# Scores and tiled outputs of two batches in one stretch, later planned landings, halves in steps 1 and 2, an earlier load of wo, last rows in two parts: one change to a fused linear-attention and feed-forward kernel

## The chip, the cores and the metric

The kernel runs on one core of one Trainium2 chip. The metric is device time in microseconds, as the median of several executions; the spans in the profiles are some 1.5 to 2 us shorter. A comparison is a ratio of the two kernels' fast runs in the same rounds on the same chip, so it is not quite the ratio of the medians that are quoted beside it. A run over 1.5% above the fastest of its kernel counts as slow and is left out. "Faster" and "slower" mean by over 2%. The "granted clock" is the share of its full clock that TensorE was given, as the trace records it. The experiments ran on several chips, so I compare ratios to the kernel before, not microseconds.

## The reference

Four batches of 768 tokens, 8 heads of 48 columns. A gated linear attention feeds a gated feed-forward.

```python
f = 1 / (1 + exp(-f_logit))
for t in range(S):                                    # S = 768
    state = f[:, :, t, :, None] * state + einsum('bhd,bhe->bhde', k[:, :, t], v[:, :, t])
    y[:, :, t] = einsum('bhd,bhde->bhe', q[:, :, t], state)
x = y.transpose(0, 2, 1, 3).reshape(3072, 384)
out = (maximum(x @ w_gate, 0) * (x @ w_val)) @ w_out  # 384 -> 1536 -> 384
```

## The kernel before

The tokens are cut in six steps c of 128. For each step, and for two batches (a pair) at a time, the inputs f, k, q, v are loaded; ScalarE makes exponentials of the running sum of log f, GpSimd scales k and q with them ("hats"), both are transposed ("qkT"), TensorE makes the scores, VectorE masks them ("ptm"), and TensorE makes the output rows ("y") from masks, v and the state. All four batches of a step then form 512 columns for the feed-forward: 12 hidden blocks j, each with a gate and a value product of three matmuls, and the output projection.

The program is written by a planner. Every operation is added with its reads, writes, a duration and a priority; a list scheduler with a model of the DMA queues fixes one order for each engine and for the DMA queue, and each engine's program is written out in that order, with a wait for whatever an operation depends on:

```python
for op in order[name]:              # one engine's program
    for d in waits[op]:             # semaphores of what it depends on
        eng.wait_ge(...)
    ins = op.emit()
```

An operation on a PSUM bank gets one of eight; groups have limits, and an operation that opens several waits until so many are idle:

```python
pl = Plan({"bc": 2, "bc4": 4, "tp": 2, "s": 4, "y": 2, "kv": 1, "f": 4})
...                                                     # cut
idle = [s for s in slots if s["tile"] is None or all(o.start is not None for o in s["tile"].ops)]
return idle[:n] if len(idle) >= n else None
```

The early loads with their gates ("wo0@q1.0": not before q of step 1, pair 0, has landed), and the planned landing:

```python
flight = 3                                              # later loads: at most three in flight
first = ("f0.0 k0.0 q0.0 v0.0 f0.1 k0.1 q0.1 v0.1 wg0@f0.1 wv0 wg1@q0.1 wv1 wg2 wv2 f1.0@wv1 k1.0 q1.0 v1.0 wo0@q1.0 wo1 wo2 "
         "f1.1 k1.1 q1.1 v1.1").split()
...                                                     # cut, in transfers():
h[0].land = t + (0.6 if e == "SP" else 1.6)
```

Scores, one batch at a time: eight matmuls of 48 rows into two banks, two heads of a pair from partitions 0 and 64 on. The outputs of steps 0 to 2 are "tiled", 28 matmuls with 32 columns of weights each:

```python
sA, sB = Bank("s"), Bank("s")
def scores():
    for p in range(NP):
        for j, s in ((0, sA), (1, sB)):
            lo = 64 * j
            mm = te.matmul(s.ap[:, p * C:(p + 1) * C], tokens(c, b, 1, p, lo, lo + D), tokens(c, b, 0, p, lo, lo + D))
    return mm
chain("scores", "PE", scores, qk_(qi), [sA, sB], occ=0.34, lat=PE_L, prio=P + 5, opens=[sA, sB])
```

## Time and profile before

| | before |
|---|---|
| median time | 199.1 us (198.9 to 199.8) |
| profiled span | 197.6 us |
| TensorE busy | 185.2 us, 94% |
| granted clock in the profiled run | 1.00 |

The busy time of the engines by stretch, kernel before. Columns: stretch, its length, then busy us (and instructions) of TensorE, its weight loads, VectorE, ScalarE, GpSimd; last the granted clock, the DMA engines' share and GB/s.

```profile
0.00:50.00 50.00, 41.65 (x467) 24.97 (x472) 32.14 (x68) 28.63 (x65) 25.83 (x46) 1.00 1.07 207
50.00:130.00 80.00, 79.16 (x822) 43.81 (x832) 49.00 (x79) 54.53 (x122) 45.66 (x57) 1.00 0.99 201
```

The reader is to see two things: TensorE is idle 8.4 us in the first 50 and only 0.8 in the next 80; and the DMA engines' share is 1.07 and 0.99, so in both stretches the transfers fill them as well (the tool's share can come out a little above 1; I read both as full). (The trace of before lacks 23 of the 512-column matmuls; each leaves, by my estimate, about 0.05 us of seeming idle time, as a recorded one lasts 0.379 us and two starts around a missing one lie 2 x 0.217 us apart; so the true idle time in the second stretch is smaller still.)

### The profile page before, as it was taken

The page shows a single profiled execution, that of the slowest core. Times are in us where ns is not written, and L with a number is a line of the kernel's source. Part 1 is how long each engine was busy: PE and PEld are TensorE (multiplying, and loading weights), DVE is VectorE, ACT ScalarE, POOL GpSimd, SP SyncE. Part 2 cuts the span into 40 slices and gives each one's busy share as a digit, 9 for nine tenths or more (in the row PEclk, how much of TensorE's full clock was granted, in tenths as well). Part 3 has the DMA queues.
Part 4 walks back from the last instruction along what each step waited for, and adds up shares of the span by engine and source line. Part 5 has one row for each costly group of instructions (what it writes and reads, how often), then busy time and mean ns, then how long its engine had stood idle before and what let it go on. Part 6 is the DMA issues. An engine that isn't in the chain of part 4 may idle for free.

```text
span 197.6 us, 4229 instructions
## 1 busy us (share of the span) xinstructions
PE 185.2 (94%) x1681; PEld 102.3 (52%) x1705; DVE 105.7 (53%) x183; ACT 111.1 (56%) x237; POOL 76.3 (39%) x108
## 2 busy tenths in 40 slices
PE   6876896898999999999999999999999999999994
PEld 1344684455655554546455555544545555544562
DVE  7746873773829786576466455446247232443300
ACT  3667429761587768856646876377434434344311
POOL 8277003956376929684730645505400000000000
PEclk9999999999999999999999999999999999999999
DMA  5999999997999999997999979989361210111112
GB/s 136 251 285 206 206 197 222 204 207 152 203 239 242 224 190 205 189 241 135 195 214 196 215 169 181 213 167 250 71 134 62 61 40 0 43 40 40 40 75 85
DMA packets 118051, 31.73 MB, mean 161 GB/s; under 512 B 111120, under 2 KB 118032, under 8 KB 118032
## 3 DMA queue, kind: packets, MB, share of 16 engines
q1 hardware_dynamic: 114048, 27.93, 65.7%
q0 software_dynamic: 3984, 3.54, 11.2%
q8 instruction: 13, 0.21, 0.4%
q14 instruction: 6, 0.05, 0.1%
HBM read 25.95 MB, written 4.72 MB: 155 GB/s over the span
## 4 chain that ended last, share of the span: by engine, by line
PE 73%; DMA 14%; SPq 7%; POOL 2%; issue 1%; ACT 0%
PE ps L829 39%; PE ps L852 22%; SPq L474 7%; DMA q_in<-in_q_dram 7%; DMA wv<-in_moe_w_val_dram 4%; DMA f_in<-in_f_logit_dram 3%; PE ps L739 3%; PE ps L766 2%; PE ps L710 1%; PE ps L659 1%; PE ps L800 1%; PE ps L776 1%; PE ps L772 1%; POOL wg L494 1%; POOL hats L699 1%
## 5 line engine op out<-in xcount | busy, mean ns | idle before, releaser
L839 DVE TENSOR_TENSOR gT<-relu,ps 128x512 bf16<-128x512 bf16 (+1 forms) x78 | 50.0, 645 | 58.1 <-PE ps L829 45.1
L835 ACT ACTIVATE relu<-ps 128x512 bf16<-128x512 f32 (+1 forms) x78 | 43.6, 563 | 28.8 <-PE ps L829 28.5
L829 PE MATMUL ps<-xT,wv 128*128 128x512 bf16 (+1 forms) x225 | 57.5, 362 | 1.3 <-DMA wv<-in_moe_w_val_dram 0.7
L829 PE MATMUL ps<-xT,wg 128*128 128x512 bf16 (+1 forms) x220 | 56.7, 362 | 0.8 <-issue 0.2
L852 PE MATMUL ps<-wo,gT 128*128 128x384 bf16 x288 | 51.4, 326 | 0.1
L744 DVE TENSOR_TENSOR ptm<-ps,tri 128x512 bf16<-128x512 f32 x48 | 30.9, 685 | 11.7 <-PE ps L739 11.7
L852 PEld LDWEIGHTS ps<-wo,gT 128*128 128x128 bf16 x288 | 27.0, 98 | 18.7
L829 PEld LDWEIGHTS ps<-xT,wg 128*128 128x128 bf16 x234 | 21.7, 98 | 19.6
L829 PEld LDWEIGHTS ps<-xT,wv 128*128 128x128 bf16 x234 | 21.1, 98 | 20.5 <-DMA wv<-in_moe_w_val_dram 1.1
L696 POOL TENSOR_TENSOR hats<-k_in,expo 128x384 bf16<-128x384 f32 x20 | 20.0, 1002 | 28.4 <-ACT expo L669 15.5
L862 ACT ACTIVATE osb<-ps 128x384 f32<-128x384 f32 x24 | 11.8, 491 | 32.1 <-PE ps L852 32.0
L699 POOL TENSOR_TENSOR hats<-q_in,expo 128x384 bf16<-128x384 f32 x20 | 19.9, 1000 | 3.1 <-DMA q_in<-in_q_dram 2.7
L550 POOL TENSOR_TENSOR st<-ssum,dec 128x384 bf16<-128x384 f32 x16 | 13.5, 846 | 9.8 <-DVE ssum L548 9.8
L731 POOL CAST vpad<-v_in 128x384 bf16<-128x384 f32 x24 | 11.9, 507 | 3.6 <-DMA v_in<-in_v_dram 3.5
L669 ACT ACTIVATE expo<-ps 128x384 f32<-128x384 f32 x20 | 9.8, 491 | 3.4 <-PE ps L662 2.6
L650 ACT ACTIVATE f_in<-f_in 128x768 f32<-128x768 f32 x10 | 8.4, 840 | 4.6 <-DMA f_in<-in_f_logit_dram 4.6
L548 DVE TENSOR_TENSOR ssum<-ps,st 128x384 f32<-128x384 f32 x16 | 8.8, 553 | 3.3 <-PE ps L800 2.9
L739 PE MATMUL ps<-qkT 48*128 48x128 bf16 x192 | 9.2, 218 | 1.0 <-ACT qkT L617 1.0
L671 ACT ACTIVATE expo<-ps 128x384 f32<-128x384 f32 x20 | 9.8, 488 | 0.0
L739 PEld LDWEIGHTS ps<-qkT 48*128 48x128 bf16 x192 | 5.4, 94 | 8.0 <-issue 4.8
L715 DVE COPY qkT<-ps 128x1024 bf16<-128x1024 bf16 x8 | 5.5, 689 | 5.6 <-PE ps L710 5.6
L652 ACT ACTIVATE bneg<-f_in 128x768 bf16<-128x768 f32 x10 | 8.4, 838 | 0.1
(73 smaller groups left out, 140.9 us busy)
## 6 DMA issues: line engine op xcount, KB each, us to landing
f_in<-in_f_logit_dram SPq DMA_DIRECT2D x12, 384.0 KB, 5.4
k_in<-in_k_dram SPq DMA_DIRECT2D x12, 384.0 KB, 5.2
q_in<-in_q_dram SPq DMA_DIRECT2D x12, 384.0 KB, 5.7
v_in<-in_v_dram SPq DMA_DIRECT2D x12, 384.0 KB, 5.4
out_dram<-osb SPq DMA_DIRECT2D x24, 192.0 KB, 2.3
wg<-in_moe_w_gate_dram POOLq DMA_DIRECT2D x3, 384.0 KB, 7.5
wv<-in_moe_w_val_dram POOLq DMA_DIRECT2D x3, 384.0 KB, 8.6
wo<-in_moe_w_out_dram POOLq DMA_DIRECT2D x3, 384.0 KB, 7.9
```

Source lines behind the costliest of these rows:

```text
L474: op = add("SP", lambda: sy.dma_start(dst, src), [], in_keys(n, c, b0, b1), occ=0.7 if both else 1.0, lat=0.9, prio=c * 100, after=after, ...
L550: add("POOL", lambda: gp.tensor_tensor(t4(s_new), t4(tmp), rate, ALU.mult), [key] + dk, [f"S{b}_{c % 2}"], prio=P + 8, **pool_t(HD))
L696: add("POOL", lambda: gp.tensor_tensor(hk, kin[:, b % 2, :, :], ex[:, 1, :].rearrange("p (h d) -> p h d", h=H), ALU.mult), in_keys("k", c, ...
L699: add("POOL", lambda: gp.tensor_tensor(hq, qin[:, b % 2, :, :], ex[:, 0, :].rearrange("p (h d) -> p h d", h=H), ALU.mult), in_keys("q", c, ...
L731: add("POOL", lambda: gp.tensor_copy(vout, vin.rearrange("p (n j) d -> p n j d", j=2)), in_keys("v", c, b, b + 1) + [f"vpad{vi}"], [f"v_{v ...
L739: mm = te.matmul(s.ap[:, p * C:(p + 1) * C], tokens(c, b, 1, p, lo, lo + D), tokens(c, b, 0, p, lo, lo + D))
L744: add("DVE", lambda j=j, s=s: ve.tensor_tensor(ptm[mi][:, j, :, :], s.ap[:, :].rearrange("p (n t) -> p n t", n=NP), mask, ALU.mult), [s, " ...
L829: mm = te.matmul(bank.ap[:, 0:n], wt[:, kt, j * 128:(j + 1) * 128], xT[xi][:, kt, n0:n1], start=(kt == 0), stop=(kt == NK - 1))
L835: add("ACT", lambda: sc.activation(relu[ri][:, 0:n], gate.ap[:, 0:n], AF.Relu), [gate], [f"relu{ri}"], prio=P, **act_t(n))
L839: add("DVE", lambda: ve.tensor_tensor(gT[gi][:, j, n0:n1], relu[ri][:, 0:n], val.ap[:, 0:n], ALU.mult), [val, f"relu{ri}"], [f"gT{gi}_{j}_ ...
L852: mm = te.matmul(o[b].ap[:, 0:DM], gT[gi][:, j, b * C:(b + 1) * C], wo[:, j, :], start=(j == 0), stop=(j == NJ - 1))
L862: add("ACT", lambda b=b, oi=oi: sc.activation(osb[oi][:, :], o[b].ap[:, 0:DM], AF.Copy), [o[b]], [f"osb{oi}"], prio=P, **act_t(DM))
```

## The change

The intent: TensorE loses time in going from the matmuls of the feed-forward into the scores (0.09 us at 103.01 us in the trace of before) and into the tiled outputs (0.10 us at 53.20), so do the scores of both batches of a pair in one stretch (steps 1 to 5; "twins" below), and the tiled outputs too (1, 2); plan landings later, so that TensorE's order does not stand before late data; give the feed-forward of steps 1 and 2 in halves of two batches for most hidden blocks, so that it can start on the first pair; store the last batch's rows in two parts, to shorten the tail; and start wo earlier. The core of the diff (signatures and renamed variables cut):

```diff
-                h[0].land = t + (0.6 if e == "SP" else 1.6)
+                h[0].land = t + (1.6 if e == "POOL" else 1.0 if h[0].ready < 1.0 else 1.9)
...
-    halves = {0: 6}
+    halves = {0: 6, 1: 8, 2: 8}
+    s_twin, y_twin = {1, 2, 3, 4, 5}, {1, 2}
-    first = ("... f1.0@wv1 k1.0 q1.0 v1.0 wo0@q1.0 wo1 wo2 f1.1 k1.1 q1.1 v1.1").split()
+    first = ("... f1.0@wv1 k1.0 q1.0 v1.0 f1.1 wo0@k1.0 wo1 wo2 k1.1 q1.1 v1.1").split()
...
-        return sum({256: 0.124}.get(n, n / 2400.0 + 0.0045) for n in cols)
+        return sum({128: 0.0566, 256: 0.109, 384: 0.1627, 512: 0.2162}[n] for n in cols)
...
-        chain("scores", "PE", scores, qk_(qi), [sA, sB], occ=0.34, lat=PE_L, prio=P + 5, opens=[sA, sB])
+        for part in ([units] if c in s_twin else [[u] for u in units]):
+            def scores(part=part):
+                for b, w, s in part:
+                    ...
+            at = [s for _, _, ss in part for s in ss]
+            chain("scores", "PE", scores, [t for _, w, _ in part for t in qk_(w % NQ)], at, occ=0.21 * len(part) + 0.22, lat=PE_L,
+                  prio=part[0][1] * 10 + 5, opens=at)
...
+        for part in ([units] if tiled and c in y_twin else [[u] for u in units]):
+            ys = [Bank("y") for _ in part]
+            ...
...
+    def ffn_end(g, b, cols):
+        for i, (n0, n1) in enumerate(cols):
+            ...      # twelve matmuls, a copy and a store for the columns n0 to n1
...
-    for item in pend:
+    for item in pend[:-1]:
         ffn_out(*item)
+    ffn_end(NC - 1, B - 1, [(0, 256), (256, DM)])
```

The decay tile also gets a contiguous layout, and an unused way of making it (a set that is empty before) goes.

## The prediction

> **What bounds the kernel now.** I read the busy table and the forty slices of the page first, then the list of waits of TensorE alone, then TensorE's timeline, where start-to-start distances tell more than durations.
>
> From the page of the kernel before:
> ```profile
> PE 185.2 (94%) x1681; PEld 102.3 (52%) x1705; DVE 105.7 (53%) x183; ACT 111.1 (56%) x237; POOL 76.3 (39%) x108
> PE   6876896898999999999999999999999999999994
> DMA  5999999997999999997999979989361210111112
> PE 73%; DMA 14%; SPq 7%; POOL 2%; issue 1%; ACT 0%
> ```
> One slice is 4.9 us. From the tenth slice on TensorE is at 9 in all but the last; before that it has holes while the DMA is full. So there are two regimes: until about 49 us TensorE waits for input, and after that (in the table of busy time by stretch 9.8 to 10.0 of each 10 us) only TensorE's own work counts. The other engines are at 39 to 56% and matter only where they let it stand idle. In the second regime a gain must take time out of TensorE's stream; in the first it must fill a hole.
>
> The waits of TensorE in the kernel before (engine, line, whom it waited for: us in total, times, longest):
> ```profile
> PE ps L659 <- ACT bneg L652: 1.8, 1, 1.8
> ...
> PE ps L710 <- POOL hats L699: 1.0, 2, 0.6
> PE ps L829 <- DMA wv<-in_moe_w_val_dram: 0.7, 2, 0.6
> PE ps L766 <- DVE ptm L744: 0.7, 1, 0.7
> ```
> The first two rows are one wait of 1.76 us at 31.2 us, and two of 0.43 and 0.56 us before the transposes at 35.6 and 48.6 us. In all three the next hidden-layer or output matmuls could have run (they run right after): the plan put the attention work first because it expected the inputs sooner. The timeline of ScalarE says the same: its first f_in activation of step 1 sat idle for 2.24 us until the transfer landed, at 29.26.
>
> The timeline of TensorE (start, us, instruction, count) shows the cost of scores:
> ```profile
> 101.62 0.81 PE L829 MATMUL ps<-xT,wg 128*128 128x512 bf16 x3
> 102.27 0.81 PE L829 MATMUL ps<-xT,wv 128*128 128x512 bf16 x3
> 103.01 0.40 PE L739 MATMUL ps<-qkT 48*128 48x128 bf16 x8
> 103.34 0.82 PE L829 MATMUL ps<-xT,wg 128*128 128x512 bf16 x3
> 104.00 0.81 PE L829 MATMUL ps<-xT,wv 128*128 128x512 bf16 x3
> ```
> Three matmuls of 512 columns take 102.27 - 101.62 = 0.65 us, but 103.01 - 102.27 = 0.74 when scores follow: 0.09 us to get into the scores. The scores take 103.34 - 103.01 = 0.33, and the three after them 0.66, so getting out is inside the 0.33. One stretch costs 0.42 us. Step 0 already has two batches back to back:
> ```profile
> 19.70 0.63 PE L739 MATMUL ps<-qkT 48*128 48x128 bf16 x16
> 20.26 0.50 PE L829 MATMUL ps<-xT,wg 128*128 128x256 bf16 x3
> ```
> Sixteen take 20.26 - 19.70 = 0.56 us, so the second eight add only 0.23.
>
> [...] the trace has 0.65/3 = 0.217 us for 512 columns, and 0.33/3 = 0.109 for 256, so halving the columns costs TensorE next to nothing. [...] The full DMA row up to 49 us agrees, and it is why moving wo earlier can't be free. [...] Here four masks of 685 ns must follow one pair of scores; see the rivals.
>
> **The change part by part.**
> Scores of two batches in one stretch, steps 1 to 5: ten pairs. Before 2 x 0.42 = 0.84, after 0.09 + 0.56 = 0.65; saved 0.19 each, 1.9 us in all, on TensorE where it is the bound (the pairs of step 1 lie in the holes, so some of it may not count).
> Tiled outputs of two batches, steps 1 and 2: four pairs. In the timeline at 53 us the output stretch of 28 runs from 53.20 to 53.71 = 0.51; its first 12 take 0.18, 0.015 each, so 28 need 0.42 and the exit 0.09. The four output-projection matmuls before it take 0.75 instead of 0.65, so the entry is 0.10. One exit and one entry per pair go: 0.19 x 4 = 0.8 us.
> Later planned landings: the code only changes an order of instructions, by planning most loads 1.3 us later. It aims at the three waits, 1.76 + 0.43 + 0.56 = 2.75 us. 1.3 of the first and all of the two short ones would be 2.3; I count 2.0, as a new order makes small holes of its own. The weights come on the other queue, whose planned landing is unchanged, so their 0.7 us stays, as do the ones before 17 us, where nothing else is ready.
> Halves in steps 1 and 2: eight of the twelve hidden columns run for two batches at a time, so step 1 can start on its first pair. This removes no work: 16 x 6 matmuls become twice as many of 256, at 2 x 0.109 - 0.217, about 0.1 to 0.2 us in all. VectorE pays 2 x 418 - 687 = 149 ns, ScalarE 2 x 382 - 596 = 168 ns, each 16 times: 2.4 and 2.7 us beside TensorE. Its worth is as filler: with the holes closed, TensorE would reach the end of step 0's output work before the second pair of step 1 is there (its q landed at 47.4 us). The half is 8 x 6 x 0.109 = 5.2 us of filler, enough for the 3 us by which TensorE comes earlier. So I book nothing for it, but the row above depends on it.
> Order of loads (f of pair 1 before wo, wo after k): the bytes are the same; 0.
> Decay layout: contiguous for the state update on GpSimd (846 ns, 16 times), off the path; 0.
> Last rows in two parts: 12 x 0.163 = 1.95 us of matmuls become 12 x (0.109 + 0.056) = 1.98. The last copy shrinks from 491 ns to about 275 (from 596 at 512 columns and 382 at 256: 0.84 ns a column). The last store is a third as large; stores took 1.8 to 4.4 us to land, median 2.3, so I take off 0.2. Together 0.4 us, all on the path, as nothing follows.
>
> Sum: 1.9 + 0.8 + 2.0 + 0.4 - 0.2 = 4.9 us. I take off 0.5 for waits that the longer stretches will bring: 199.1 - 4.4 = **194.7 us**.
>
> **The rivals.**
> (a) PSUM banks. Twin scores need four of eight banks at once, while the feed-forward may hold four. If TensorE has to wait for them, up to the 0.19 per pair is given back and more. Speaking for it: between 60 and 80 us VectorE is busy 16.0 of 20 us, the halves add some 2 us there, and four masks in a row are 2.7 us. Against it: the plan knows these durations, and with four banks of its own TensorE has two column blocks, 2.6 us, to work on meanwhile. If it comes true in steps 1 and 2, 1 to 2 us are lost: about 196.
> (b) The input is the bound until 49 us anyway. Then closing the holes early only moves them to 50-57 us, where TensorE waits for the second pair of step 1: the 2.0 us vanish and some of step 1's saving too, about 197. For it: the DMA row is full there. Against: the halves give 5.2 us of other work, and after 57 us TensorE never starves.
> (c) All holes in the first regime close, the weights' too, and all twins pay in full (from finer starts nearer 0.22 each): 3.1 + 2.75 + 0.7 + 0.4, about 192.3.
>
> **Range and chances.** 192.4 (rival c) to 197.0 (rival b). Faster by 2% means below 195.2, and my figure is 0.5 us on the good side of it with a spread of about 1.6: 0.61. Slower by 2% needs a wait of 8 us, far above any in this trace: 0.03.
>
> **What would show it.** TensorE's count of scores stretches of 8 falls and stretches of 16 take about 0.56 from steps 1 to 5; the waits on L652's and L699's successors shrink below 1 us together; TensorE's busy time falls by 2.5 to 3 us (the switches are booked as busy) and its idle time by about 2; from the last matmul to the end is 0.4 us shorter. The prediction is wrong if TensorE has new waits for masks (ptm), for gT or for q_in between 48 and 80 us, or if step 1's second pair comes late.

## The result, and the profile after

The changed kernel takes 202.0 us (201.2 to 202.5, 4 runs) against 199.1 (198.9 to 199.8, 4 runs): ratio 1.0135, 95% interval 1.0092 to 1.0178. That is within 2%, but on the slow side, and outside the predicted range.

The profile after, from the page: busy times, then TensorE, its granted clock and the DMA in forty slices of 5 us.

```profile
PE 188.0 (94%) x1814; PEld 115.8 (58%) x1814; DVE 105.8 (53%) x199; ACT 112.9 (56%) x254; POOL 75.9 (38%) x108
PE   6978999809999999999999999999999999999995
PEclk9996999985999999999999999999999999999999
DMA  5999999999389898999987897997954111111113
```

TensorE's holes before 40 us have closed as predicted, but the ninth slice is 0: it stands still. And the clock is granted at 8 and 5 tenths in slices nine and ten. TensorE's busy time went up by 2.8 us, not down by 2.5 to 3. Two things hide what the change took out of its work. Of its work 3.40 and 5.50 us ran at half clock, where output matmuls took twice as long (0.32 us for 0.163, see below), which makes 4.5 us too many; and the 23 missing records take some 1.2 us from the figure of before. Estimated from these, the work itself went from 185.2 + 1.2 = 186.4 us to 188.0 - 4.5 = 183.5, or 2.9 us down, as predicted. The waits of TensorE in the kernel after:

```profile
PE ps L723 <- ACT relu L839: 5.3, 1, 5.3
...
PE ps L657 <- ACT bneg L650: 0.4, 1, 0.4
```

The three waits that the later landings aimed at (1.76, 0.43 and 0.56 us) are gone, though not through the landings, as e6 will show; one of 5.3 us has come. Follow it back. TensorE's timeline after:

```profile
38.65 0.81 PE L833 MATMUL ps<-xT,wv 128*128 128x512 bf16 x3
44.80 1.03 PE L723 MATMUL ps<-qkT 48*128 48x128 bf16 x16 [5.34 <-ACT relu L839]
...
46.81 4.54 PE L876 MATMUL ps<-wo,gT 128*128 128x384 bf16 x16
```

The paired scores of step 1 wait for a relu on ScalarE, which must empty a PSUM bank. ScalarE's timeline after says why the relu is late; below it, the row of the same activation in the kernel before:

```profile
43.33 0.84 ACT L648 ACTIVATE f_in<-f_in 128x768 f32<-128x768 f32 x1 [7.71 <-DMA f_in<-in_f_logit_dram]
44.08 0.58 ACT L839 ACTIVATE relu<-ps 128x512 bf16<-128x512 f32 x1
```

```profile
36.05 0.84 ACT L650 ACTIVATE f_in<-f_in 128x768 f32<-128x768 f32 x1 [1.32 <-DMA f_in<-in_f_logit_dram]
```

The relu stands in ScalarE's queue behind the exponential of f of step 1, pair 1, which waited 7.71 us for its transfer. The load was issued at about the same time in both kernels; SyncE's DMA queue before, then after:

```profile
30.46 1.59 SPq L474 DMA_DIRECT2D f_in<-in_f_logit_dram  x1
```

```profile
30.53 2.22 SPq L472 DMA_DIRECT2D f_in<-in_f_logit_dram  x1
```

But it was there by 36.05 us before and by 43.33 after: 5.6 us became 12.8. The other queue's issues tell the difference; GpSimd's timeline before, then after:

```profile
32.71 0.81 POOL L494 DMA_DIRECT2D wo<-in_moe_w_out_dram  x1 [14.14 <-DMA q_in<-in_q_dram]
35.88 1.55 POOL L494 DMA_DIRECT2D wo<-in_moe_w_out_dram  x2
```

```profile
30.45 2.26 POOL L492 DMA_DIRECT2D wo<-in_moe_w_out_dram  x3 [12.23 <-DMA k_in<-in_k_dram]
```

Before, the first part of wo starts 2.2 us after f and the other two when f is nearly there; after, all three (384 KB each) start with it. In the changed kernel's own plan this f was to land at 37.6 us, 5.7 us too early.

In the standstill, from 39.5 to 44.8 us, the clock drops too. In stretches of 0.2 us the granted clock is still 1.00 up to 43.6 us, 4.1 us into the standstill, and then 0.50 until 50.4 us: 6.8 us in all, 5.6 of them after TensorE's next matmul (44.80). From 46.8 us on output matmuls start 0.32 us apart (0.163 in the rest of the trace). The trace also has half clock from 16.3 to 19.7 us, after three waits of 0.5 to 0.8 us close together and no long standstill: in the 4.1 us before, TensorE was busy for 2.52. What brought the clock down there is not shown. That stretch comes and goes: the traces of e5 and e13 have it too (0.66 on average from 15 to 20 us), most others have full clock there. (The mean clock is 0.974 to 0.983 in the changed kernel's four runs, 0.98 to 1.0 in those of before.)

What the change was built for did happen. Scores of two batches, TensorE's timeline after, later in the run:

```profile
109.98 0.81 PE L833 MATMUL ps<-xT,wv 128*128 128x512 bf16 x3
110.72 0.62 PE L723 MATMUL ps<-qkT 48*128 48x128 bf16 x16
111.28 0.82 PE L833 MATMUL ps<-xT,wg 128*128 128x512 bf16 x3
```

The pair takes 111.28 - 110.72 = 0.56 us and 110.72 - 109.98 - 0.65 = 0.09 us to get in: the 0.65 of the prediction, for 0.84 before. And the tail; the chain that ended last, before and after:

```profile
186.91 7.81 PE ps L852 x48
194.73 0.02 issue
194.75 0.49 ACT osb L862
```

```profile
195.70 1.99 PE ps L856 x24
197.69 0.02 issue
197.72 0.28 ACT osb L861
```

The second copy is of 128 columns in place of 384. From the last matmul in the chain to the end of the span it was 197.6 - 194.73 = 2.9 us and is 200.0 - 197.69 = 2.3.

### The profile page after: what moved, and what is told of

Same layout as the page of the kernel before.

```text
span 200.0 us, 4531 instructions
## 1 busy us (share of the span) xinstructions
PE 188.0 (94%) x1814; PEld 115.8 (58%) x1814; DVE 105.8 (53%) x199; ACT 112.9 (56%) x254; POOL 75.9 (38%) x108
## 4 chain that ended last, share of the span: by engine, by line
PE 72%; DMA 16%; SPq 7%; ACT 3%; issue 1%; POOL 0%
PE ps L833 36%; PE ps L876 23%; DMA f_in<-in_f_logit_dram 9%; SPq L472 7%; DMA wv<-in_moe_w_val_dram 4%; DMA q_in<-in_q_dram 3%; PE ps L723 2%; PE ps L657 2%; PE ps L758 2%; PE ps L693 1%; PE ps L809 1%; PE ps L770 1%; ACT relu L839 1%; PE ps L856 1%; PE ps L766 1%; ACT f_in L648 1%
## 5 line engine op out<-in xcount | busy, mean ns | idle before, releaser
L843 DVE TENSOR_TENSOR gT<-relu,ps 128x512 bf16<-128x512 bf16 (+1 forms) x94 | 51.5, 559 | 56.0 <-PE ps L833 36.1
L839 ACT ACTIVATE relu<-ps 128x512 bf16<-128x512 f32 (+1 forms) x94 | 46.1, 496 | 29.7 <-PE ps L833 29.3
L833 PE MATMUL ps<-xT,wg 128*128 128x512 bf16 (+1 forms) x282 | 62.8, 332 | 0.0
L833 PE MATMUL ps<-xT,wv 128*128 128x512 bf16 (+1 forms) x282 | 62.5, 331 | 0.0
L833 PEld LDWEIGHTS ps<-xT,wv 128*128 128x128 bf16 x282 | 26.6, 98 | 17.8
L833 PEld LDWEIGHTS ps<-xT,wg 128*128 128x128 bf16 x282 | 26.5, 99 | 16.2
L886 ACT ACTIVATE osb<-ps 128x384 f32<-128x384 f32 x23 | 11.3, 490 | 29.6 <-PE ps L876 29.3
L723 PE MATMUL ps<-qkT 48*128 48x128 bf16 x192 | 7.9, 224 | 6.1 <-ACT relu L839 5.3
```

Of the source, the lines that this page charges most:

```text
L723: mm = te.matmul(s[j].ap[:, p * C:(p + 1) * C], tokens(c, b, 1, p, lo, lo + D), tokens(c, b, 0, p, lo, lo + D))
L833: mm = te.matmul(bank.ap[:, 0:n], wt[:, kt, j * 128:(j + 1) * 128], xT[xi][:, kt, n0:n1], start=(kt == 0), stop=(kt == NK - 1))
L839: add("ACT", lambda: sc.activation(relu[ri][:, 0:n], gate.ap[:, 0:n], AF.Relu), [gate], [f"relu{ri}"], prio=P, **act_t(n))
L843: add("DVE", lambda: ve.tensor_tensor(gT[gi][:, j, n0:n1], relu[ri][:, 0:n], val.ap[:, 0:n], ALU.mult), [val, f"relu{ri}"], [f"gT{gi}_{j}_ ...
L886: add("ACT", lambda b=b, oi=oi: sc.activation(osb[oi][:, :], o[b].ap[:, 0:DM], AF.Copy), [o[b]], [f"osb{oi}"], prio=P, **act_t(DM))
```

## The experiments

Eighteen runs were made, of seventeen kernels (e17 is e7 again). "Old loads" below means the early loads' order and gates as before.

### 1. Is it the early wo?

Theory L: wo, started earlier, rides with f and delays it, ScalarE's queue stands behind f, TensorE behind ScalarE. Theory B: the paired scores wait for four banks, whatever the loads do.

**e1_old_loads**: the changed kernel with

```diff
-  "... q1.0 v1.0 f1.1 wo0@k1.0 wo1 wo2 k1.1 q1.1 v1.1"
+  "... q1.0 v1.0 wo0@q1.0 wo1 wo2 f1.1 k1.1 q1.1 v1.1"
```

> The changed kernel, with the order and gates of the early loads as before (wo after q of step 1, not after k). Theory L (loads): wo moved earlier rides with f of the second pair of step 1, whose landing goes from 36 to 43 us; ScalarE's queue stands behind it, TensorE with it, and the clock drops. Without it f lands before 37.5 us, the 5.3 us wait of TensorE before the scores is under 1 us, the granted clock is 1.0 after 20 us, and the time is 193.5 to 195.5 us. Theory B (banks): the scores of two batches need four PSUM banks at once and wait for them whatever the loads do; then a wait of 3 us or more stays before L723 and the time is above 199.

Measured: 200.33 us, ratio 1.0064 (1.0026 to 1.0103), clock 1.0. f is there at 36.37 us and the 5.3 us wait is gone, as theory L has it, but the time is 5 us above what I expected. Its waits, longest first:

```profile
PE ps L876 <- DMA wo<-in_moe_w_out_dram: 2.0, 2, 1.2
PE ps L833 <- DMA xT<-xn: 1.5, 1, 1.5
PE ps L693 <- POOL hats L682: 1.4, 3, 0.9
...
PE ps L833 <- DMA wv<-in_moe_w_val_dram: 1.2, 2, 0.6
```

None is long. Most end in a DMA, and the first lies at 43 to 47 us: with the early holes closed, TensorE reaches the output projection before wo has landed.

**e2_new_loads_only**: the kernel before with the new order and gates of the early loads alone.

> The kernel before, with only the new order and gates of the early loads. Theory L: f of the second pair of step 1 lands near 43 us here too, ScalarE waits for it for 4 us or more and the time goes up by 2 to 7 us (201 to 206), as nothing pays for it. Theory B: the load order is harmless with single scores; within 1 us of before (198 to 200).

Measured: 201.14 us, 1.0125 (1.0076 to 1.0173). The loads alone cost the kernel before as much as the whole change. Not as I expected, ScalarE waits only 1.0 us for f (at 43.00): in this kernel the plan itself put f at 41.3 us and gave ScalarE other work. (So the plan's model of the queues can see that wo delays f; with the changed kernel's other times it put f at 37.6.) The late f costs time without the long wait.

**e3_single_scores**: the changed kernel with `s_twin = set()`.

> The changed kernel, with the scores of one batch at a time again (two banks). Theory L: ScalarE still waits about 7 us for f, TensorE still stands for 3 us or more between 36 and 46 us (it can go one or two stretches further on two banks), and the time is 201.5 to 204.5, as the twins' 2 us are lost too. Theory B: the wait is gone and the time is 196 to 198.

Measured: 204.42 us, 1.0255 (1.0205 to 1.0305). Scores on two banks do not help; TensorE's queue then stands at the running sums, which need the same f:

```profile
PE ps L657 <- ACT bneg L650: 5.1, 1, 5.1
```

So four banks are not the cause of the long wait; theory B falls for it.

**e4_plan_f_late**: the changed kernel, transfers untouched, with the plan told that this f lands 5.7 us later.

```diff
                 self.transfers()
+                for op, more in self.later.items():      # later = {f1.1: 5.7}
+                    op.land += more
```

> The changed kernel with its loads, but the plan is told that f of the second pair of step 1 lands 5.7 us later than it reckons (at 43.3, as the trace has it), so that ScalarE takes other work first. The transfers stay as they are. If the harm is the order on ScalarE's queue (relu behind the waiting exponential), TensorE's long wait shrinks below 1.5 us, the clock stays at 1.0 and the time is 195 to 197.5, a little over e1 as step 1's second pair is late all the same. If the harm is the late data itself, the wait moves to another place and the time stays above 199.5.

Measured: 200.37 us, 1.0069 (1.0038 to 1.0099), clock 1.0. TensorE's longest wait is 1.5 us: the order on ScalarE's queue made the long wait (in the ACT rows of the changed kernel above the relu runs at 44.08 us, right after the activation on f at 43.33). But the time misses my 195 to 197.5 and equals e1's.

Over all twenty traces, before and after included, there are two kinds and nothing between: where all wo is issued from 30.2 to 32.2 us (after, e2, e3, e4, e18), the activation on f starts at 43.0 to 43.5; where the first wo goes out after 32.3 (the other fifteen), at 35.2 to 36.9.

So undoing the early wo, or planning for it, brings back 0.7% of the 1.35%. The other 5 us that I had predicted are still missing.

### 2. Which part costs what

**e5_no_halves**: e1 with `halves = {0: 6}`.

> The kernel of the first run (changed, with the old loads; 1.006 of before) without halves in steps 1 and 2. Its trace has scores of step 2 start at 72 us against 61 before, and TensorE out of feed-forward work at 111 us, waiting 1.5 us for xT. Theory H: the many small halves take each bank as it comes free and run the feed-forward ahead, so the pair of scores finds four banks late; then the scores of step 2 start before 66 us here, and the time is 197.5 to 199. Theory T: the twins alone need their four banks and are late without halves too: after 68 us, time 199.5 to 201.

Measured: 200.46 us, 1.0047 (1.0005 to 1.0090). The scores of step 2 do start at 61.5 us instead of 72, as theory H has it, but the time is that of e1 within the intervals. The halves delay the scores and that delay is not what costs.

**e6_old_landings**: e1 with the landing line of before.

> The kernel of the first run with the planned landings as before. If the later landings close the holes before 50 us as predicted (2.0 us), this is slower: 1.012 to 1.018 of before (201.5 to 203). If TensorE is held by the input until 49 us whatever the order, the waits only come back at their old places and the time is within 0.8 us of the first run's 200.3, or better.

Measured: 200.93 us, 1.0090 (1.0055 to 1.0124), against e1's 1.0064 on another chip. The second expectation holds: the later landings are worth 0.5 us or nothing here, not 2.0. Nor is it they that closed the three waits. With the old landing line, e6's trace has 0.23, 0.23 and no wait at their places, and one of 0.83 us for a relu beside the first: 1.3 us in all from 24 to 50 us. In e1, with the later landings, TensorE waits there for 0.87, 0.84, 1.20 and 0.23 us, 3.1 in all, against 2.75 in the kernel before.

**e7_twin_scores_only** and, the same kernel again, **e17_twin_again**: the kernel before with twin scores alone (old loads and landings, no halves, single outputs, one last store).

> The kernel before with scores of two batches in one stretch in steps 1 to 5 and nothing else (old loads, old landings, no halves, single outputs, one last store). If only the switches of TensorE count: 2 us less, 196.8 to 197.8. If the pair comes late for want of four banks at once (theory T) or of the second batch: the gain is eaten, 198.7 to 200.5, with scores of step 2 several us later than 61.

> The twins-only kernel once more, unaltered. As before: 1.000 to 1.006 of before. If supply theory S holds, its twin with halved loads (0.9899) stays at least 0.8% below it. If the difference was one of chips, this comes out at 0.992 or less.

Measured: 199.66 us, 1.0030 (0.9990 to 1.0070) on one chip; 198.06 us, 0.9963 (0.9931 to 0.9995) on another. The first profile fell on the slowest execution of its six (201.2), so I don't read it. The kernel gains between nothing and 0.4% where 1.0% was saved on TensorE, and between the two chips it moves by 0.7%, where the kernel before moves by 0.2% (199.14 and 198.75 us). e17 lies outside both of its expectations: it is better than 1.000 to 1.006, and not as good as the 0.992 that would have made chips the cause.

**e8_end_only** and **e9_end_exact**: the last rows in two parts alone. In e8 it is the changed program with every other part switched off, planned anew; in e9 it is the program of before, and the order of all operations up to the last projection stays what it was.

> The kernel before with only the last rows in two parts (and the decay layout). From the last matmul to the end the trace has 3.2 us before and 2.5 changed, so 0.6 us less if that part stands alone: 0.9955 to 0.998 of before. If the shorter tail is not on the path: 0.999 to 1.001.

> The kernel before with only the last batch's rows in two parts, written so that the order of every earlier instruction stays exactly that of before (the other end-only kernel had its whole order planned anew). The tail is on the path and TensorE's stream is untouched: 0.5 to 0.7 us less than before, 0.9965 to 0.9975. If this is reached, then the earlier run's 1.0027 was the price of the new order, not of the tail; if it too stays at 1.00 or above, the tail itself gains nothing.

Measured: e8 199.56 us, 1.0027 (0.9983 to 1.0071), inconclusive. e9 198.30 us, 0.9975 (0.9954 to 0.9995): the 0.5 us of the tail. (The 3.2 and 2.5 us in the expectation count from the start of the last matmul, the 2.9 and 2.3 above from its end.) In e8's trace the tail is as short, but TensorE's last matmul ends 2.8 us later than before, after new waits at 59 us (1.2 us, for the padded v) and 122 us (0.9 us, for a transposed qkT). That profile too fell on the slowest of its six executions (201.6 us, the others 198.7 to 199.8), so it shows that the new plan, with its changed cost table and order of adding, has other waits, and not what they cost. That the new order eats the tail's gain is likely and not shown: the intervals of e8 and e9 overlap, and they ran on different chips.

### 3. Is it the supply of inputs?

By now the saved time turned into small waits, mostly after 50 us. Theory S: from 50 to 130 us the inputs come no faster than TensorE of the kernel before used them, so what TensorE saves it waits. Theory O: the planned orders make the waits. To tell them apart I halved the loads from the second pair of step 2 on: only 64 of 128 rows are read, in the same order of instructions. The result is wrong (relative error 0.6); the program has no branch on the values, and I take it that the wrong values alone change no time (not shown separately).

```diff
             dst = t[:, slot, :, :, :].rearrange("p b h d -> p (b h) d")
+            if 2 * c + b0 // 2 >= 5:       # src likewise: 64 rows
+                dst = t[0:64, slot, :, :, :].rearrange("p b h d -> p (b h) d")
```

**e10_before_half_loads**, **e11_e1_half_loads**, **e12_twin_half_loads**:

> Wrong result on purpose: the kernel before, same order, but every load of f, k, q, v from the second pair of step 2 on brings only half of the rows (the rest is what lay there). Reference for the next two. Before has only about 1 us of idle TensorE after 50 us, so at most 1 us faster: 0.994 to 1.0.

> Wrong result on purpose: the first run's kernel (changed, old loads) with the same halved loads, same order. Theory S (supply): after 50 us the inputs come no faster than before, so the time that TensorE saves turns into waits (3.4 us after 50 us in the first run against 1.0 before); then these waits fall below 1 us and the time goes from 200.3 to 196.5 to 198. Theory O (order): the waits come from the planned order of each engine and of the DMA queue, not from the transfers' size; they stay at 2.5 us or more and the time stays within 1 us of 200.3.

> Wrong result on purpose: the kernel before with twin scores alone (199.66 in its own run) with the halved loads, same order. Theory S: with the supply relieved the 2 us of saved switches show, 196.8 to 197.8. Theory O: the waits for the transposed qkT (1.6 us) stay and the time is 198.7 to 200.

| | full loads | halved loads |
|---|---|---|
| before | 1 | 0.9994 (0.9974 to 1.0014) |
| twins only | 1.0030, 0.9963 | 0.9899 (0.9877 to 0.9921) |
| e1: all but the early wo | 1.0064 | 0.9856 (0.9822 to 0.9891) |

The halving gives the kernel before nothing and e1 about 2%: 195.84 us, even below the 196.5 to 198 of theory S. The busy times by stretch of e1, then of e11:

```profile
50.00:130.00 80.00, 76.47 (x914) 52.76 (x922) 50.05 (x95) 53.72 (x134) 45.80 (x58) 1.00 0.98 196
```

```profile
50.00:130.00 80.00, 79.36 (x939) 54.93 (x946) 50.73 (x97) 57.59 (x142) 45.78 (x58) 1.00 0.76 144
```

With full loads TensorE is idle 80 - 76.47 = 3.5 us there, and the DMA share is 0.98; with halved loads, in the same order, 0.6 us at 0.76. Theory S holds, if the supply is taken as what the DMA engines carry in all: the longest wait of e1 in this stretch, 1.5 us at 113.5 us, is for a transposed x (xT), which they write too, and it is gone in e11. Whether the inputs themselves or the transposes beside them came late, no run separates. (e1 and e11 ran on different chips; the 2.1% between their ratios is three times the spread that e7 and e17 show between chips.) The twins alone now save 1.0%, the 1.9 us of the prediction. The evidence from the twins is weaker than that from e1, though: e17's expectation asked for at least 0.8% between full and halved loads, and it is 1.3% against e7 but only 0.6% against e17.

**e18_after_half_loads**: the changed kernel itself, with the same halving.

> Wrong result on purpose: the changed kernel, its own loads up to step 2, later loads halved. Its trace has hardly any idle TensorE after 50 us (0.4 us to 130), as the 5.3 us wait let the inputs get ahead. If the long wait stands in for the later waits, halving has nothing to remove here: 201 to 202.3, against the 4.5 us that it took from the first run's kernel. If the later inputs hold this one too: below 199.5.

Measured: 200.73 us, 1.0099 (1.0068 to 1.0131), between the two expectations, nearer the first; the interval overlaps that of the changed kernel (1.0135). Its wait and its second stretch:

```profile
PE ps L727 <- ACT relu L843: 5.3, 1, 5.3
```

```profile
50.00:130.00 80.00, 80.00 (x978) 54.85 (x977) 47.62 (x92) 55.80 (x137) 45.82 (x58) 0.99 0.66 135
```

The 5.3 us and the low clock are untouched, and from 50 to 130 us there was hardly a wait to remove (0.4 us in the changed kernel, at full loads). So, across two chips, the early wo costs 1.0099 - 0.9856 = 2.4%, near 5 us, where the supply is relieved, and only 1.0135 - 1.0064 = 0.7% where it is not: most of what the long wait costs would otherwise have been spent in waits that the supply forces later.

### 4. Can more loads in flight give the supply?

**e13_e1_flight5**, **e14_twin_end_flight5** (before with twins and the new end) and **e15_before_flight5**: `flight = 5` for 3.

> The first run's kernel (changed, old loads, 1.006 of before) with five loads in flight in place of three. If the number in flight limits the supply: the waits after 50 us (3.5 us) fall below 1.5 and the time is 196.5 to 198.5. If the transfers' own cost does, as the DMA row at 9 from 50 to 130 us suggests: within 0.8 us of 200.3.

> The kernel before with twin scores, the last rows in two parts and five loads in flight. If the number in flight limits the supply: 196.3 to 197.8, better than both kernels. If the transfers' cost does: 198.3 to 200, the twins' gain still eaten.

> Control: the kernel before with five loads in flight. It has hardly a wait after 50 us, so either way 0.997 to 1.004 of before.

Measured: 0.9992 (0.9944 to 1.0039), 0.9956 (0.9917 to 0.9994) and 0.9966 (0.9927 to 1.0005). The control, with hardly a wait to lose after 50 us, gained about as much as e14 and came out a little better than I expected, so this tells nothing for certain. e13 and e14 fit neither of their expectations: e14 (198.16 us) falls just between the two, and e13 (198.95 us) is better than e1 by 0.7%, but on another chip, and its TensorE is still idle 2.9 us from 50 to 130 us with the DMA share at 1.03. The supply looks set by what the transfers cost more than by their number; that is argued, not shown.

**e16_end_flight5**: the order of before, the last rows in two parts, five in flight.

> The kernel before with the last rows in two parts and five loads in flight, nothing else. If the two gains are independent, as they lie at opposite ends of the run: 0.9975 x 0.9966 = 0.994 of before, about 197.7. If the flight gain was chance: 0.997 to 0.998.

Measured: 198.08 us, 0.9970 (0.9944 to 0.9995). Not the sum; the flight's part was chance or too small to see. The versions that give right results and whose whole interval lies below 1 are e14, e16 and e9, at 0.9956 to 0.9975 of before, with intervals too wide to rank them (e17 too, at 0.9963, but the same kernel gave 1.0030 as e7). All three are ahead of the kernel before by less than half a per cent, and of the changed one by about 1.7%.

## Why the prediction was wrong, point by point

| step of the prediction | predicted | shown by |
|---|---|---|
| scores of pairs | 1.9 us less TensorE work | 0.65 for 0.84 us in the trace; 1.0% in e12. At full loads 0 to 0.4% (e7, e17) |
| tiled outputs of pairs | 0.8 us less | a pair's stretch takes 0.89 us in TensorE's timeline (62.52 to 63.41) for two of 0.51, and one entry of 0.10 goes: 0.23 a pair; not run alone |
| later planned landings | 2.0 us less | e6 against e1: 0.5 us or nothing; the three waits go without the landings too |
| halves | 0, as a filler | e5 against e1: no difference |
| order of loads | "the bytes are the same; 0" | 0.7% in the change (e1, e4), 1.25% alone (e2), 2.4% with supply relieved (e11, e18) |
| last rows in two parts | 0.4 us less | 0.5 us (e9) |
| waits from longer stretches | 0.5 us more | near 3 us more idle time in e1 from 50 to 130 us (3.5 for 0.8), from the supply (e11) |

**The first step that failed** is "the bytes are the same; 0". The bytes are, but not who gets them first. The prediction itself had named the full DMA row as "why moving wo earlier can't be free", and then booked zero. It could be seen: f of pair 1 went out at 30.46 us and the first wo at 32.71, and the change moves wo's gate from q to k, a load earlier. In the changed kernel the plan's model of the queues missed it too, by 5.7 us, and everything that the plan put behind f on ScalarE stood still (7.71 us), and TensorE with it (5.34 us).

**The second** is "after that only TensorE's own work counts". TensorE's idle 0.8 us from 50 to 130 us was read as its being the bound alone. The DMA row says 9 there as well; two engines were full, and I read that row only up to 49 us. Rival (b), "the input is the bound until 49 us anyway", named the right cause and set its end 80 us too early. With the supply relieved, e11 is 2.9 us below the kernel before (195.84 for 198.76 on its chip), which is the prediction's 1.9 + 0.8 + 0.4 - 0.2 for TensorE's own work: these sizes were right as a sum, and their being worth as much at full loads was not. That e11 falls within the range of the prediction is in part luck, as the 2.0 us for later landings are not in it. That term failed by itself: in e1, TensorE, let through earlier, waits for wo at 43 to 47 us, and the old landing line (e6) leaves it less idle before 50 us, not more.

**Rival (a)**, the four banks, is real as a delay (the scores of step 2 start at 72 us in e1, 61.5 without halves) and costs nothing that the runs show.

**The remark that the prediction would be wrong "if step 1's second pair comes late"** was right: its scores started at 57.9 us, 50.4 before. What I had not foreseen is the clock: half speed for the work from 44.8 to 50.4 us, by the estimate above some 2.8 us of TensorE's time.

What stays open: how much of the changed kernel's loss is the clock alone, since part of its 2.8 us may, like the wait, stand in for later waits; whether the transfers' cost or the order on the DMA queue sets the supply from 50 to 130 us; and what the tiled outputs are worth by themselves.

## What to carry to other kernels

Before you book a saving on an engine that is never idle, look whether a second row, the DMA's above all, is full in the same slices; if it is, a saving on the first alone may come back as waits, as it did here (in e1 TensorE was idle for 3.5 us from 50 to 130 us, against 0.8 before), and halving the transfers in the same order of instructions (a wrong result) shows it in one run (0.6 us of idle time in e11). A transfer moved earlier can make somebody else's later, as wo did f here (12.8 us for 5.6): find which small, awaited load it will ride with, and what stands behind that load in its engine's order (here a relu of 0.58 us, for which TensorE stood still for 5.3). And where a planner writes the program, test one part with the order of everything else kept, since a new order alone may cost as much as the part gains (e8 against e9 differ by half a per cent here, with intervals that overlap).
